# An expert kernel whose work is ordered by a list scheduler instead of by written times

## The chip, the core and the metric

The kernel runs on one core of one Trainium2 chip. The metric is the time of one execution on the device, in microseconds (us); a smaller number is better. Before the change, three runs took 2221.42 to 2222.93 us, with a median of 2222.36 us.

The core has five engines that matter here. TensorE (PE in the profile) multiplies matrices into PSUM. VectorE (DVE), ScalarE (ACT) and GpSimd (POOL) do the elementwise work. SyncE (SP) only issues transfers between HBM and SBUF here. Each engine works through its own queue strictly in the order in which the program issued its instructions, and waits on semaphores for the results of the others. So the order in which the program is written decides what an instruction that waits holds up behind it.

## What is computed

The reference is causal attention with a decay, then a dense mixture of experts, then a two-layer network. Cut to what matters:

```python
x = attention(q, k, v, f)            # 4 x 8 heads, 576 tokens each, head size 64 -> (2304, 512)
P = sinkhorn(exp(x @ w_gate), 8)     # 8 rounds of row and column normalisation, (2304, 8)
out = 0
for e in range(8):                   # every token goes through every expert
    h = maximum(x @ w1[e], 0)        # (2304, 1024)
    out += P[:, e:e+1] * (h @ w2[e])
h = out @ w_in                       # (2304, 2048)
return maximum(0.01 * h, h) @ w_out
```

All matrices are float32. The kernel keeps that precision by splitting each operand into a high and a low half and multiplying three times (high by high, high by low, low by high).

## The kernel before

Attention comes first, some 326 us long, and is the same in both versions. Into its gaps, and after it, go "fills": the products of the first four halves of experts for the first third of the tokens. What follows works on units.

**Units.** The tokens stand in three parts of 768, the hidden columns in groups of 512: 16 groups `g` for the experts (two per expert) and 4 for the last network (stage 1, from `GE` = 16 on). A unit is one part with one group, and there are 56 (part 0 skips the groups that the fills did). A unit's two matrix products are done by Strassen's scheme, so each layer takes 7 products of half size instead of 8: `p1` to `p7` for the first layer, `l1` to `l7` for the second. Each is 12 matmuls of 128x384 on TensorE. The products of unit u stand between the second-layer products of unit u-1, in the fixed order of `Q`: p1 p2 l1 p6 l2 l6 p7 p5 l5 l7 p3 p4 l3 l4. This order is the same after the change.

**Around the products.** ScalarE copies three products out of PSUM (`keep`, L1052), VectorE adds and applies the activation and the row of P (`c_add`, `act`, L1055 to L1071), GpSimd forms four sums (`s_sum`, L1078), ScalarE rounds each operand of the second layer to its high half (`op_hi`, L1083), VectorE subtracts to get the low half (`op_lo`, L1087), and the results are added into the accumulators (`evict`, L1095 on VectorE, L1093 on ScalarE for a first visit). Weights go the same way: raw load (L150), sums on VectorE (`w_sum`, L846), high half on ScalarE (L161), low half on GpSimd (L162). The operands of the first layer are made once per stage and part: four sums (`x_sum`, L774), seven high halves (`x_hi`, L777), seven low halves (`x_lo`, L781), then stores to HBM (`x_out`, L784 and L785); units load them back (`x_get`, L1014). For stage 1 they are made from the finished accumulators. The weights of the last network arrive as 64-bit words and are rewritten as float32 in 64 pieces (`conv_a`, L889 and L890; `conv_square`, L894; `conv_b`, L899 and L900).

**What sets the order.** Every event is entered with a time that its author computed from the nominal start of the products and a few durations, `at(t, key, name, fn, ..., need=...)`. At the end of the program each event is moved behind the last of its needs by a thousandth, and all are issued in order of these times:

```python
when[x] = max(when[x], last + 1e-3)
...
for t, x, key, name, fn, args, need in sorted(todo, key=lambda x: (when[x[2:4]], x[1])):
    fn(*args)
```

Nothing in this knows that an engine can do only one thing at a time, nor how long a transfer takes.

## Time and profile before

| | |
|---|---|
| median of three runs | 2222.36 us |
| the profiled execution, its own time | 2222.18 us |
| its span, first to last instruction | 2220.4 us |
| TensorE busy | 2055.6 us (93%) |
| VectorE busy | 1779.7 us (80%) |
| GpSimd busy | 1124.7 us (51%) |
| ScalarE busy | 984.0 us (44%) |
| the chain of work that ended last | TensorE 57%, VectorE 20%, GpSimd 7%, transfers 4% |

The profile is of one execution; its own time lies within the three runs. TensorE's share of busy time is an average over parts of the program with different limits. How much TensorE loses is read stage by stage: from the length of a stretch against the work in it.

### The profile page before, as it was taken

To read this page: it belongs to the slowest core of one execution; us is meant where nothing else is said; L and a number is where in the kernel's file an instruction comes from. 1 tells how busy PE (TensorE), PEld (TensorE's weight loads), DVE (VectorE), ACT (ScalarE), POOL (GpSimd) and SP (SyncE) were. 2 spreads that over 40 slices of the span, in tenths; PEclk is the share of its full clock that TensorE was granted. 3 is DMA by queue.
4 is the path that set the end of the run, shared out by engine and by line. 5 is a ranking of instruction groups with operands and counts; after the bars stand their busy time and mean duration, and the time that the engine had idled before them with its cause. 6 is when DMAs were issued, how large, how long until landed. Compare 5 with 4: busy or idle time off the path is not lost.

```text
span 2220.4 us, 32472 instructions
## 1 busy us (share of the span) xinstructions
PE 2055.6 (93%) x11760; PEld 1974.8 (89%) x11760; DVE 1779.7 (80%) x2257; ACT 984.0 (44%) x1784; POOL 1124.7 (51%) x709
## 2 busy tenths in 40 slices
PE   7999997699899999999999999999999877988998
PEld 6888886589889999999899999999999867888998
DVE  6789856487878888988889889889888766889656
ACT  7888854254333333333333333333333334544443
POOL 4676644376545545445454454543545445444531
PEclk9999999899999999999999999999999988999999
DMA  5655535857766676666676676766666777666653
GB/s 137 167 150 152 138 108 192 302 180 241 277 248 227 235 243 227 234 234 228 232 234 219 241 234 224 247 237 222 235 214 239 256 257 257 218 232 238 217 196 133
DMA packets 153798, 482.87 MB, mean 217 GB/s; under 512 B 16824, under 2 KB 43080, under 8 KB 153640
## 3 DMA queue, kind: packets, MB, share of 16 engines
q1 hardware_dynamic: 153640, 480.80, 64.0%
q8 instruction: 94, 1.54, 0.3%
q14 instruction: 64, 0.52, 0.1%
HBM read 424.78 MB, written 51.22 MB: 214 GB/s over the span
## 4 chain that ended last, share of the span: by engine, by line
PE 57%; DVE 20%; issue 8%; POOL 7%; DMA 4%; ACT 3%; SPq 1%; POOLq 0%; DVEq 0%; ACTq 0%
PE x L1027 28%; PE y L1027 18%; DVE acc_C L1095 3%; DVE wr L846 3%; PE ps_pv L529 3%; POOL w L162 3%; DVE hl L1087 2%; POOL s L1078 2%; PE ps_m L228 2%; PE ps_t L493 2%; POOL k L1078 1%; PE ps_m L201 1%; DVE u L1069 1%; DVE y L1055 1%; PE ps_s L441 1%
## 5 line engine op out<-in xcount | busy, mean ns | idle before, releaser
L162 POOL TENSOR_TENSOR w<-wr,w 128x512 fp32r<-128x512 f32 x288 | 417.8, 1456 | 457.0 <-ACT w L161 402.1
L1027 PE MATMUL x<-hh,w 128*128 128x384 f32 x1792 | 508.9, 345 | 80.2 <-DVE acc_C L1095 56.4
L1027 PE MATMUL x<-xw,w 128*128 128x384 f32 x2676 | 512.1, 340 | 13.2 <-ACT u L1052 4.5
L1027 PEld LDWEIGHTS x<-xw,w 128*128 128x128 f32 x2676 | 475.1, 191 | 23.2 <-ACT u L1052 10.8
L1027 PEld LDWEIGHTS x<-hh,w 128*128 128x128 f32 x1792 | 336.4, 193 | 95.3 <-DVE acc_C L1095 56.3
L1027 PE MATMUL y<-xw,w 128*128 128x384 f32 x2004 | 379.7, 337 | 18.1 <-DVE u L1058 16.2
L1027 PEld LDWEIGHTS y<-xw,w 128*128 128x128 f32 x2004 | 350.6, 189 | 25.2 <-DVE u L1058 23.0
L1027 PE MATMUL y<-hh,w 128*128 128x384 f32 x1344 | 368.4, 334 | 0.0
L1027 PE MATMUL x<-hl,w 128*128 128x384 f32 x896 | 306.2, 342 | 1.6 <-DVE hl L1087 1.6
L1078 POOL TENSOR_TENSOR k<-k,u 128x768 f32<-128x768 f32 x55 | 102.2, 1858 | 348.0 <-DVE u L1069 262.5
L1027 PEld LDWEIGHTS y<-hh,w 128*128 128x128 f32 x1344 | 245.1, 188 | 0.2 <-DVE acc_C L1095 0.2
L1027 PE MATMUL y<-hl,w 128*128 128x384 f32 x672 | 224.6, 334 | 0.0
L161 ACT ACTIVATE w<-wr 128x512 fp32r<-128x512 f32 x288 | 178.2, 622 | 75.5 <-PE y L1027 33.2
L1083 ACT ACTIVATE hh<-c 128x768 fp32r<-128x768 f32 x112 | 94.3, 842 | 217.8 <-PE y L1027 101.6
L1095 DVE TENSOR_TENSOR acc_C<-y,acc_C 128x768 f32<-128x768 f32 x148 | 140.6, 950 | 53.2 <-PE y L1027 53.2
L1095 DVE TENSOR_TENSOR acc_C<-x,acc_C 128x768 f32<-128x768 f32 x178 | 168.9, 949 | 9.9 <-PE x L1027 9.3
L1027 PEld LDWEIGHTS x<-hl,w 128*128 128x128 f32 x896 | 173.4, 194 | 2.0 <-DVE hl L1087 2.0
L1052 ACT ACTIVATE u<-x 128x768 f32<-128x768 f32 x112 | 91.0, 812 | 173.3 <-DVE hl L1087 137.4
L1083 ACT ACTIVATE hh<-u 128x768 fp32r<-128x768 f32 x112 | 94.1, 840 | 126.0 <-PE y L1027 108.6
L1087 DVE TENSOR_TENSOR hl<-u,hh 128x768 fp32r<-128x768 f32 x112 | 121.6, 1085 | 32.1 <-ACT hh L1083 32.1
L1087 DVE TENSOR_TENSOR hl<-s,hh 128x768 fp32r<-128x768 f32 x56 | 95.4, 1704 | 59.1 <-ACT hh L1083 58.9
L1087 DVE TENSOR_TENSOR hl<-c,hh 128x768 fp32r<-128x768 f32 x112 | 136.9, 1222 | 4.9 <-ACT hh L1083 2.6
(222 smaller groups left out, 3546.6 us busy)
## 6 DMA issues: line engine op xcount, KB each, us to landing
xw<-xo_t SPq DMA_DIRECT2D x224, 768.0 KB
xw<-xo_b SPq DMA_DIRECT2D x166, 768.0 KB
wr<-in_w_dram SPq DMA_DIRECT2D x88, 512.0 KB
pb<-prow SPq DMA_DIRECT2D x44, 384.0 KB
rq<-in_qT_dram SPq DMA_DIRECT2D x64, 144.0 KB
rk<-in_kT_dram SPq DMA_DIRECT2D x64, 144.0 KB
...
```

What stands on the lines that cost most here:

```text
L161: nc.scalar.activation(hv, src, AF.Copy)
L162: nc.gpsimd.tensor_tensor(lv, src, f(hv), ALU.subtract)
L228: nc.tensor.matmul(ps, h_[:, ts], w_, start=(x == 0), stop=(x == 11))
L493: nc.tensor.transpose(ps[:KV[j], c:c + m], prb[n, i][:m, j * P:j * P + KV[j]], ident[:m, :m])
L529: nc.tensor.matmul(ps[:, a - ra:rb - ra], vp, s[:KV[j], o:o + rb - a], start=(x == 0), stop=(x == len(todo) - 1))
L846: nc.vector.tensor_tensor(o, x, y, op)
L1027: nc.tensor.matmul(o_, w[:, k, w_], m[:, k, :], start=a and k + y == 0, stop=z and k == 1 and y == 2, skip_group_check=True)
L1052: nc.scalar.activation(ctile(u, name, name, bufs), pview(u, p), AF.Copy)
L1078: (nc.vector if u == NU - 1 else nc.gpsimd).tensor_tensor(tmp[u, o], tmp[u, a], tmp[u, b], op)
L1083: nc.scalar.activation(hi, tmp[u, LSRC[l]], AF.Copy)
L1087: nc.vector.tensor_tensor(lo, tmp[u, LSRC[l]], f(hi), ALU.subtract)
L1095: nc.vector.tensor_tensor(a, pview(u, l), a, ALU.add)
```

## The change

The times written for each event are replaced by a description of what the event is. `ev` takes an engine and a duration (`how`), all events that must come first (`need`), and events whose start it must follow (`after`). The letters are M for TensorE, A for ScalarE, V for VectorE, P for GpSimd and D for the transfers; "VP" marks a VectorE operation that can't run beside one on GpSimd, and a second pair in `how` lets the scheduler choose the engine. `run_events` computes a due time for every event backwards from the nominal places of the products. Then it walks forward through a model of five engines: it takes the candidate that can start first, looks past it to a more urgent one that becomes ready within its length, and issues the program in the order so found. The products keep their order among themselves.

Some events are cut finer or placed elsewhere. A fill's matmuls and the two halves of its rounding are events of their own. The high and low halves of the weights are two events. The loads of x of parts 1 and 2 have no need and so come at the start of this phase, part 1 first (before: part 2 at the start, part 1 some 34 us ahead of the first unit, after all stores of part 2). GpSimd may take any sum or low half of x. Of the 64 conversion pieces 48 instead of 40 lie in the stretch of units 9 to 41, evenly spaced, and 16 instead of 24 behind.

```diff
-    todo = []
-
-    def at(t, key, name, fn, *args, need=()):
-        todo.append((t, len(todo), key, name, fn, args, need))
-
-    HOP = 0.15
+
+
+
+    ENG = dict(V=nc.vector, P=nc.gpsimd)
+    TM, TMF1, TMF2 = 2.08, 0.70, 0.89
+    VX = ("V", 0.97)
+    VS = ("VP", 0.98)
+    VF = ("VP", 0.98, "P", 1.9)
+    AX_ = ("A", 0.85)
+    PX = ("P", 1.88)
+    DX = ("D", 1.95)
+    HOP, LAND = 0.13, 2.0
+    LOOK = dict(A=1.0, V=1.0, P=1.0, D=1.0)
...
+    def run_events():
...
+        for x, (_, _, _, need, after, _, _) in evs.items():
+            if evs[x][5] > noms[0]:
+                after.append(line[min(bisect_left(noms, evs[x][5]), len(line) - 1)])
...
+        due = {}
+        for x in reversed(topo):
+            how, due_ = evs[x][0], evs[x][6]
+            d = place.get(x, 1e9 if due_ is None else due_)
+            if x not in place:
+                for y, hard in succ[x]:
+                    lag = how[1] + HOP + (LAND if how[0] == "D" else 0.0) if hard else 0.0
+                    d = min(d, due[y] - lag)
+            due[x] = d
...
+        def offer(x):
+            how, _, _, need, after, t, _ = evs[x]
+            r = 0.0
+            me = how[0][0]
+            for n in need:
+                e = ran[n]
+                r = max(r, over[n] + (LAND if e == "D" else 0.0) + (0.03 if e == me else HOP))
+            for n in after:
+                r = max(r, at_[n])
+            for e in how[0::2]:
+                cand[e[0]][x] = (r, due[x], e == "VP" or e == "P")
+
...
+        order = []
+        while len(order) < len(evs):
+            best = None
+            for e in free:
+                here = []
+                for x, (r, d, p) in cand[e].items():
+                    if e == "M" and x in place and x != line[nl[0]]:
+                        continue
+                    s_ = max(r, free[e])
+                    if p:
+                        s_ = max(s_, port["P" if e == "V" else "V"])
+                    here.append((s_, e == "M" and x in place, d, e == "P", x))
+                if not here:
+                    continue
+                here.sort(key=lambda k: k[:4])
+                k = here[0]
+                if e in LOOK:
+
+                    for y in here[1:]:
+                        long = dur_of(k[4], e)
+                        if y[2] < k[2] and y[0] < k[0] + LOOK[e] * long and y[2] + slip[0] < k[0] + long:
+                            k = y
+                if best is None or k[:4] < best[0]:
+                    best = (k[:4], k[4], e)
+            k, x, e = best
+            how = evs[x][0]
+            if e == "M":
+                if x in place:
+                    nl[0] += 1
+                    slip[0] = k[0] - place[x]
+            for c in cand.values():
+                c.pop(x, None)
+            dur = dur_of(x, e)
+            at_[x], ran[x] = k[0], e
+            over[x] = free[e] = k[0] + dur
+            if how[0] == "VP" or e == "P":
+                port[e] = over[x]
+            order.append(x)
+            for y, _ in succ[x]:
+                left[y] -= 1
+                if not left[y]:
+                    offer(y)
+        for x in order:
+            how, fn, args = evs[x][:3]
+            fn(*args, *((ran[x],) if len(how) > 2 else ()))
 
...
+            need = [made[m] for m in XFROM[n]] + [(X, m) for m in XOVER[n]]
+            ev(X, n, VF if flex else VS, x_sum, stage, part, n, need=need)
+            made[n] = (X, n)
+        for n in XOPS:
+            to = (lambda n=n: xlo[n]) if n in near else (lambda: None)
+            ev(X, "h " + n, AX_, x_hi, stage, part, n, need=[made[n]] + list(free.get(n, ())))
+            ev(X, "l " + n, VF if flex else VS,
+               lambda *e, n=n, to=to: x_lo(stage, part, n, to(), *(e or ("V",))),
                need=[(X, "h " + n)] + [(X, m) for m in XLAST[n]])
...
+            ev(X, "o " + n, DX, lambda n=n, to=to: x_out(stage, part, n, to()), need=[(X, "l " + n)])
...
-    T0X = {2: 1.0, 1: base - 34.0}
-    for part in (2, 1):
-        t0, X = T0X[part], ("x", 0, part)
-        was = lambda n, m=None: [(("x", 0, 2), "o " + n)]
-        pre = [(("x", 0, 2), "o " + n) for n in XOPS] if part == 1 else []
-        at(t0, X, "load", x_load, part, BLK, need=[("start", "places")] + pre)
-        free = dict(t3=[(X, "o b11")], t1=[(X, "o b21")], b22=[(X, "o t2")], t4=[(X, "o t3")])
-        if part == 1:
-            free = dict(b22=[(X, "o t2")], t4=[(X, "o t3")])
-        x_events(0, part, t0 + 4.0, {n: (t0 + 4.0, (X, "load")) for n in BLK},
-                 4.5 if part == 2 else 2.6, free, "vvpvpvp")
...
+    for part in (1, 2):
+        X = ("x", 0, part)
+        for n in ("b11", "b12", "b21", "b22"):
+            ev(X, "load " + n, ("D", 1.1), lambda part=part, n=n: x_block(part, n, xat[0, part][n]))
+        free = dict(t2=[], t3=[], t1=[], b22=[(X, "o t2")], t4=[(X, "o t3")])
+        if part == 2:
+            was = lambda n: [(("x", 0, 1), "o " + n)]
+            free = dict(b11=was("b22"), b21=was("t4"), t2=was("t1"), t3=[(X, "o b11")],
+                        t1=[(X, "o b21")], b22=[(X, "o t2")], t4=[(X, "o t3")])
+        x_events(X, True, free, {n: (X, "load " + n) for n in BLK}, ("b11", "b21") if part == 1 else ())
+        if part == 2:
+            for n in ("t2", "t3", "t4"):
+                evs[X, n][3].extend(was(n))
...
-    cu = []
-    for u in range(9, U2 - 2):
-        cu += [(u, 0)] + ([(u, 1)] if u % 5 == 0 else [])
-    for u in range(U2 + 2, U2 + 8):
-        cu += [(u, x) for x in range(5)]
-    for j, (u, x) in enumerate(cu[:64]):
...
+    n1 = 48
+    for j in range(64):
+        ct.append(unit0[9] + span * j / n1 if j < n1 else unit0[U2 + 2] + 8.0 * (j - n1))
...
-        at(ta - 8.0, C, "load", conv_load, j, need=need)
-        at(ta, C, "a", conv_a, j, need=[(C, "load")])
-        at(ta + 2.0, C, "square", conv_square, j, need=[(C, "a")])
-        at(ta + 6.1, C, "b", conv_b, j, need=[(C, "square")])
...
+        ev(C, "load", ("D", 0.75), conv_load, j, need=need, t=ct[j] - 8.0)
+        ev(C, "a", ("V", 0.72), conv_a, j, need=[(C, "load")], t=ct[j])
+        ev(C, "square", ("A", 0.4), conv_square, j, need=[(C, "a")])
+        ev(C, "b", ("V", 0.86), conv_b, j, need=[(C, "square")])
+        ev(C, "store", ("D", 0.4), conv_store, j, need=[(C, "b")])
...
+                need = [dep(d) for d in WDEP[str(x)]] + [(G, f"raw {which}")]
+                need += w_free(14 * g + 7 * which + x)
+                ev(G, f"{nm}hi {x}", ("A", 0.64), w_high, g, which, x, need=need, after=[wlast],
+                   t=t_ + gap * x)
+                ev(G, f"{nm}lo {x}", ("P", 1.3), w_low, g, which, x, need=[(G, f"{nm}hi {x}")])
+                wlast = (G, f"{nm}hi {x}")
...
+                ev(G, f"{nm}s{x}", ("VP", 0.7), w_sum, g, which, x, need=need)
...
+        need = [(("x", g // GE, part), "o " + XN[p])] + ([lastf[0]] if x < XR else [loads[x - XR]])
+        after = [(loads[x - 1][0], "x " + loads[x - 1][1])] if x else []
+        ev(u, "x " + p, DX, x_get, u, p, need=need, after=after)
...
-            at(E_[u, l] + HOP, key, "e " + l, evict, u, l, need=need)
...
+            if g not in (0, GE) or l in ("l2", "l3", "l7"):
+                need += [(key, "e " + dict(l2="l1", l3="l6", l7="l5").get(l, l))] if l in ("l2", "l3", "l7") else []
+            first = g in (0, GE) and l in ("l1", "l6", "l5", "l4")
+            ev(key, "e " + l, AX_ if first else VX, evict, u, l, need=need,
+               due=E_[u, l] + 3.0)
...
-    for t, x, key, name, fn, args, need in sorted(todo, key=lambda x: (when[x[2:4]], x[1])):
-        assert did.issuperset(need), (key, name, need)
-        fn(*args)
-        did.add((key, name))
```

**ScalarE at the end of the fills**, as the queue of before holds it. `hh<-` are the high halves that a fill's second layer waits for; the rows from `xu_4897` to `xc_4900<-acc_C_1_4876` are the seven high halves of x of part 1.

```order
L166 ACTIVATE hh<-y_5271 128x384
L973 ACTIVATE acc<-acc,prob 128x512
L161 ACTIVATE w<-wr 128x512
L777 ACTIVATE xu_4897<-acc_C_1_4873 128x768
L777 ACTIVATE xs_4899<-acc_C_1_4874 128x768
L777 ACTIVATE acc_C_0_4871<-spare_4882 128x768
L777 ACTIVATE acc_C_0_4872<-acc_C_1_4875 128x768
L777 ACTIVATE xc_4900<-spare_4881 128x768
L777 ACTIVATE acc_C_0_4871<-spare_4883 128x768
L777 ACTIVATE xc_4900<-acc_C_1_4876 128x768
L166 ACTIVATE hh<-x_5298 128x384
L166 ACTIVATE hh<-y_5360 128x384
```

The same place after the change (`L902` is `x_hi`, `L214` the fill's high half, `acc_C_2` belongs to part 2):

```order
L1093 ACTIVATE acc<-acc,prob 128x512
L1075 ACTIVATE pr<-x_5212 72x256
L1093 ACTIVATE acc<-acc,prob 128x512 x2
L163 ACTIVATE w<-wr 128x512
L1093 ACTIVATE acc<-acc,prob 128x512 x3
L902 ACTIVATE xc_4887<-acc_C_1_4876 128x768
L214 ACTIVATE hh<-y_5278 128x384
L902 ACTIVATE xc_4887<-acc_C_2_4877 128x768
L214 ACTIVATE hh<-x_5297 128x384
L214 ACTIVATE hh<-y_5317 128x384
L214 ACTIVATE hh<-x_5335 128x384
L163 ACTIVATE w<-ws 128x512
```

Before, seven halves of x stand in one block ahead of two fills; after, the halves of part 1 are mostly earlier, and one of part 1 and one of part 2 stand between fills.

**VectorE in the slot of unit 18**, a typical one in the long middle. Before: `L1095` adds a product into an accumulator, `L1087` is a low half, `L889` and `L890` are a conversion's first two operations, `L1055` and `L1069` belong to p2; the row with `x_10391` for `acc_C_0_4871` is the one that l1 of the unit before gives, and that l6 waits for.

```order
L1095 TENSOR_TENSOR acc_C_2_4878<-y_10237,acc_C_2_4878 128x768
L1087 TENSOR_TENSOR hl<-c_10327,hh 128x768
L1095 TENSOR_TENSOR acc_C_2_4879<-x_10117,acc_C_2_4879 128x768
L1087 TENSOR_TENSOR hl<-s_10342,hh 128x768
L889 TENSOR_SCALAR acc<-acc 128x256
L890 SCALAR_TENSOR_TENSOR acc<-acc 128x256
L1055 TENSOR_TENSOR y_10372<-y_10372,k_10389 128x2x384
L1069 SCALAR_TENSOR_TENSOR k_10389<-y_10372,pb 128x768
L1095 TENSOR_TENSOR acc_C_0_4871<-x_10391,acc_C_0_4871 128x768
L1087 TENSOR_TENSOR hl<-u_10173,hh 128x768
```

After (`L1217` adds, `L1209` is a low half, `L998` and `L999` are the conversion, `x_10398` is l1):

```order
L1217 TENSOR_TENSOR acc_C_2_4878<-y_10235,acc_C_2_4878 128x768
L998 TENSOR_SCALAR acc<-acc 128x256
L999 SCALAR_TENSOR_TENSOR acc<-acc 128x256
L1217 TENSOR_TENSOR acc_C_2_4879<-x_10121,acc_C_2_4879 128x768
L1008 SCALAR_TENSOR_TENSOR acc<-acc 128x256
L1009 SCALAR_TENSOR_TENSOR acc<-acc 128x256
L1209 TENSOR_TENSOR hl<-c_10328,hh 128x768
L1209 TENSOR_TENSOR hl<-s_10349,hh 128x768
L1177 TENSOR_TENSOR y_10376<-y_10376,k_10391 128x2x384
L1191 SCALAR_TENSOR_TENSOR k_10391<-y_10376,pb 128x768
L1217 TENSOR_TENSOR acc_C_0_4871<-x_10398,acc_C_0_4871 128x768
L1209 TENSOR_TENSOR hl<-u_10193,hh 128x768
```

The conversion has moved ahead of the last addition of the unit before, its second half (`L1008`, `L1009`) follows at once, and nothing of it stands any more between the low half for l6 (`hl<-s`) and the addition of l1.

**ScalarE at the border of the two stages**, in the slot of unit 45, from the copy of p1 on. Before: `L777` rows are high halves of x of part 2, `L1093` is the first visit of l1 to its accumulator.

```order
L1052 ACTIVATE k_17781<-x_17742 128x768
L777 ACTIVATE acc<-spare_4881 128x768
L1071 ACTIVATE k_17781<-y_17766 128x768
L777 ACTIVATE acc<-spare_4882 128x768
L1083 ACTIVATE hh<-u_17552 128x768
L1093 ACTIVATE acc_C_0_4871<-x_17789 128x768
L161 ACTIVATE w<-wr 128x512
```

After (`L902` is a high half of x, `L1215` the first visit):

```order
L1174 ACTIVATE k_17769<-x_17739 128x768
L902 ACTIVATE acc<-spare_4883 128x768
L1205 ACTIVATE hh<-s_17772 128x768
L1193 ACTIVATE k_17769<-y_17756 128x768
L1215 ACTIVATE acc_C_0_4871<-x_17777 128x768
L1205 ACTIVATE hh<-u_17588 128x768
L163 ACTIVATE w<-ws 128x512
```

Two high halves of x stood ahead of l1's first visit to its accumulator; now one does, the last of part 1, and behind it comes the high half for l6 (`hh<-s`).

## Rows read from the trace of the kernel before

**Rows 1.** The page: length of the profiled span.
```profile
span 2220.4 us, 32472 instructions
```
**Rows 2.** Stretches: length; busy PE, PEld, DVE, ACT, POOL; clock, DMA share, GB/s.
```profile
326.00:404.35 78.35, 53.12 (x259) 45.84 (x259) 45.18 (x91) 28.42 (x48) 32.59 (x21) 0.87 0.64 226
404.35:474.82 70.47, 57.40 (x292) 53.56 (x292) 48.27 (x44) 25.61 (x41) 38.52 (x23) 0.93 0.62 221
474.82:701.29 226.47, 213.57 (x1202) 210.32 (x1201) 176.77 (x183) 95.96 (x136) 132.02 (x79) 0.98 0.71 251
701.29:1741.41 1040.12, 1007.14 (x5713) 989.82 (x5713) 907.37 (x963) 374.72 (x538) 514.86 (x294) 1.00 0.67 232
1741.41:2051.51 310.10, 256.98 (x1345) 247.32 (x1345) 240.88 (x269) 136.36 (x203) 148.36 (x83) 0.92 0.70 242
2051.51:2168.04 116.53, 116.53 (x673) 116.53 (x673) 71.43 (x74) 52.13 (x67) 52.35 (x29) 1.00 0.60 209
```
**Rows 3.** What TensorE waited for, 326 to 474.82: total us, times, longest.
```profile
PE x L201 <- DVE hl L167: 17.8, 1, 17.8
PE x L1027 <- ACT hh L1083: 4.6, 1, 4.6
```
**Rows 4.** Timeline of ScalarE: start, length, instruction, idle time before it and its releaser.
```profile
398.24 0.84 ACT L777 ACTIVATE xc<-acc_C 128x768 fp32r<-128x768 f32 x1 [5.65 <-DMA xo_t<-xc]
398.99 0.47 ACT L166 ACTIVATE hh<-x 128x384 fp32r<-128x384 f32 x1
```
**Rows 5.** Timeline of TensorE around that wait.
```profile
380.41 2.38 PE L201 MATMUL y<-xp,w 128*128 128x384 f32 x12 [1.24 <-DVE hl L167]
400.60 3.92 PE L201 MATMUL x<-xp,w 128*128 128x384 f32 x12 [17.80 <-DVE hl L167]
```
**Rows 6.** What TensorE waited for, 701.29 to 1741.41.
```profile
PE x L1027 <- DVE acc_C L1095: 21.8, 26, 1.6
PE y L1027 <- DVE u L1058: 10.8, 14, 2.4
```
**Rows 7.** Timeline of VectorE in the slot of unit 18.
```profile
980.85 1.38 DVE L889 TENSOR_SCALAR acc<-acc 128x256 uint32<-128x256 uint32 x1
982.26 1.95 DVE L890 SCALAR_TENSOR_TENSOR acc<-acc 128x256 uint32<-128x256 uint32 x1
986.00 0.95 DVE L1095 TENSOR_TENSOR acc_C<-x,acc_C 128x768 f32<-128x768 f32 x1
```
**Rows 8.** Timelines of TensorE and GpSimd in the same slot.
```profile
987.00 0.45 PE L1027 MATMUL x<-hh,w 128*128 128x384 f32 x1 [0.95 <-DVE acc_C L1095]
980.06 2.02 POOL L162 TENSOR_TENSOR w<-wr,w 128x512 fp32r<-128x512 f32 x1
```
**Rows 9.** Lines L1087 and L889 over the span: shortest, median, longest in ns.
```profile
L1087 DVE TENSOR_TENSOR hl<-k,hh x112: 941/958/1769, 440.1 to 2206.4; 128x768 fp32r<-128x768 f32 x112
L1087 DVE TENSOR_TENSOR hl<-c,hh x112: 941/959/2677, 441.0 to 2208.5; 128x768 fp32r<-128x768 f32 x112
L1087 DVE TENSOR_TENSOR hl<-u,hh x112: 941/959/2132, 455.6 to 2210.5; 128x768 fp32r<-128x768 f32 x112
L1087 DVE TENSOR_TENSOR hl<-s,hh x56: 946/1714/2602, 449.6 to 2199.3; 128x768 fp32r<-128x768 f32 x56
L889 DVE TENSOR_SCALAR acc<-acc x64: 281/1378/1939, 705.9 to 2044.0; 128x256 uint32<-128x256 uint32 x64
```
**Rows 10.** What TensorE waited for, 1741.41 to 2051.51.
```profile
PE x L1027 <- DVE acc_C L1095: 23.1, 8, 7.3
PE x L1027 <- ACT acc_C L1093: 15.5, 2, 12.1
```
**Rows 11.** Timelines of the transfers' queue and of ScalarE, slot of unit 45.
```profile
1848.36 0.42 SPq L784 DMA_DIRECT2D xo_b<-acc  x1
1854.22 0.84 ACT L777 ACTIVATE acc<-spare 128x768 fp32r<-128x768 f32 x1 [4.18 <-DMA xo_b<-acc]
1855.70 0.79 ACT L1093 ACTIVATE acc_C<-x 128x768 f32<-128x768 f32 x1
```

More of the change, by code (lines that the diff above doesn't have):

```diff
@@ L1165, in moe_kernel @@
             if n == "f":
-                for y, fn in enumerate(fills[n_f][1]):
-                    at(t, "start", f"fill {n_f}" + (f" {y}" if y else ""), fn)
-                t += 0.87
-                at(t + 0.6, "start", f"fill {n_f} end", fill_end)
-                ends.append(t)
-                n_f += 1
+                p_ = moved.pop(0)
+                fixed.append((t, len(fixed), p_[2]))
+                t += TMF2
                 continue
@@ L1181, in moe_kernel @@
     unit0[NU + 1] = t
-    assert n_f == nf
-    tp_ = base + 0.5
-    at(tp_, "start", "prob t", prob_t, need=[("start", "cols 7")])
-    at(tp_ + 0.7, "start", "prob out", prob_out, need=[("start", "prob t")])
-    for i in range(TPP):
-        x = nf - 1 - 3 * (TPP - 1 - i) - (3 * FC if i < TPB else 0)
-        at(ends[x] + 3.0, "start", f"scale {i}", acc_scale, i,
-           need=[("start", "cols 7"), ("start", f"fill {x} end")])
+    assert not moved
+    st = [f(cp.tile([P, 2, TB], F32R, tag=n, name="x" + n, bufs=b)) for n, b in
+          (("u3", 2), ("u3", 2), ("s2", 1), ("c21", 1), ("u2", 1))]
@@ L1400, in moe_kernel @@
-    done = set()
-    def settle(x, path=()):
-        assert x not in path, path
-        if x not in done:
-            last = max((settle(n, path + (x,)) for n in needs[x]), default=-1e9)
-            when[x] = max(when[x], last + 1e-3)
-            done.add(x)
-        return when[x]
-    for _, _, key, name, _, _, _ in todo:
-        settle((key, name))
-    did = set()
-    for t, x, key, name, fn, args, need in sorted(todo, key=lambda x: (when[x[2:4]], x[1])):
-        assert did.issuperset(need), (key, name, need)
-        fn(*args)
-        did.add((key, name))
+                ev(key, "put " + n, ("D", 1.1), put, part, n, need=[(key, "e " + l)])
@@ L1419 @@
+    run_events()
 _OUTS = [((DM, N), "float32")]
```

517 lines of the change are left out of this document (291 added, 226 removed).

## The prediction

> **What bounds the kernel now.** I read the page's header first, then the busy time by stretch, then what TensorE waited for in each stretch, and last the timelines around the longest waits. The span is 2220.4 us [rows 1], and the execution took 2222.18 us, so 1.8 us lie outside it. The three runs shown have a median of 2222.36 us, 0.2 us from the profiled one, so sums against the profile carry over as they are.
>
> The table by stretch [rows 2] is the key. Its last row is four units in which TensorE is busy for 116.53 of 116.53 us at full clock: a unit without any stall is 116.53 / 4 = 29.13 us. The products and their order on TensorE don't change, so no unit gets shorter than that. The gap of each other stretch is its length less the work in it:
>
> - A, end of attention and fills (326 to 404): 78.35 - 53.12 busy = 25.2 us idle, and a slow restart: twelve matmuls of a fill took 3.92 us after the long wait against 2.38 us earlier [rows 5], 1.5 us. Gap 26.7.
> - B, first two units with the last fills: 70.47 long, 57.40 busy at a mean clock of 0.93. The work at full clock is about 57.40 x 0.93 = 53.4. Gap 17.1.
> - C, units 2 to 8: 226.47 - 7 x 29.13 = 22.6.
> - D, units 9 to 42: 1040.12 - 34 x 29.13 = 49.7, or 1.46 per unit.
> - E, units 43 to 50 at the border of the stages: 310.10 - 8 x 29.13 = 77.1.
>
> Together 193.2 us, so with every gap closed the time is 2222.2 - 193.2 = 2029. Only these gaps are at stake; attention and the last units are left alone.
>
> **The change part by part.** Each term has the same bounds from the rows: at best its whole gap goes, at worst nothing does; a loss is possible too and has its own bound below (VectorE), so it is not repeated at each term.
>
> *A.* TensorE waited 17.8 us in one wait for a fill's low half on VectorE [rows 3]. VectorE was not the cause: its operand, the high half on ScalarE, ran at 398.99, right behind the last high half of x, which had itself waited 5.65 us for a store [rows 4]. Seven high halves of x stood ahead of two fills' halves in one queue, and the x halves wait for stores to free their buffers. After, they are spread between the fills, the raw x comes earlier, and at the last fills one half of part 1 and one of part 2 remain. The latter reuses a buffer that a store must leave first. The planner allows such a transfer 1.95 + 2.0 = 3.95 us; the trace shows 1848.36 to 1854.22 = 5.9 us from issue to release [rows 11]. What is late next is this half, by 5.9 - 3.95 = 2 us. The other 7.4 us of idle time are short waits such as the 1.24 us of [rows 5]; I leave 3. Gain 26.7 - 5 = about 22.
>
> *B.* Here the waits are for the same family of halves (4.6 us once [rows 3]) while the x work of part 2 goes on beside two units. The planner sees both, but not the true length of a transfer. I keep a third: gain 17.1 - 5.6 = 11.5. A restart at a lower clock goes with the wait before it.
>
> *C.* The same x work thins out here. By D's rate after the change (below, 0.6 per unit) 4.2 would remain; the x halves that go on beside these units make it twice that. Gain 22.6 - 8.6 = 14.
>
> *D.* TensorE waited 26 times, 21.8 us in all, for an addition on VectorE (L1095), the one of l1 that l6 must follow, and 14 times, 10.8 us, for a sum in the first layer [rows 6]. In unit 18 the cause stands in the timeline: a conversion's two operations, 1.38 and 1.95 us, run ahead of the addition at 986.00 [rows 7], and TensorE starts at 987.00 after 0.95 us of waiting [rows 8]. The new order puts the conversion ahead of the previous unit's last addition, and nothing of it between the low half for l6 and l1's addition. So the 21.8 go where a conversion was in the way. What is queued behind it now is that last addition and the low halves for l2 and l6; and the conversion's second half waits for ScalarE's square. With the second half no longer than the first (3.33 us, my bound), a piece delays them by 6.7 us. l2 is the fifth product of the slot, so four products of 29.13 / 14 = 2.08 us, 8.3 us, lie before it: covered by 1.6 us. If that cover fails, a wait of 1 to 2 us comes back per piece, 48 to 96 us over 48 pieces at the extreme; the gap before the change (1.46 per unit) speaks against it. The stretch also gets 48 pieces instead of 40: 8 x 6.7 / 34 = at most 1.6 us more of VectorE per unit on 907.37 / 34 = 26.7, so 28.3, still below 29.13. That leaves little slack, so I don't take all: of 1.46 per unit 0.6 stays. 34 x 0.6 = 20 stay; gain 49.7 - 20 = 30.
>
> The plan books a conversion's first operation with its second, at 0.72 us, as a plain VectorE event; the row has a median of 1.378 for the first alone, and a shortest of 0.281 [rows 9]. The long ones lie beside GpSimd's work: in unit 18 a weight's low half of 2.02 us ran from 980.06 [rows 8] over the 1.38 at 980.85 [rows 7]. The Trainium skill, "SBUF — State Buffer", section "Who interferes with whom", says that a VectorE operation with two SBUF inputs contends with a GpSimd operation that reads SBUF, that one in a two-port mode (a tensor_scalar can be) contends too, and that the later one then blocks for the whole instruction; these rows agree. By that rule the pieces stay long wherever the plan lets them run beside GpSimd, which is the reason for what I leave, and rival 2 if it spreads.
>
> *E.* Two things add up. ScalarE's first visit of l1 stood behind two high halves of x of which one waited 4.18 us for a store [rows 11]; TensorE waited 15.5 us in two such waits, and 23.1 in eight for the additions on VectorE [rows 10]. VectorE was busy for 240.88 / 8 = 30.1 us per unit [rows 2], over the 29.13 that TensorE needs: it bounds this stretch. After, 8 pieces fewer lie here, 8 x 3.33 to 8 x 6.7 = 27 to 54 us off VectorE, 23 to 27 us per unit, and GpSimd may take sums and low halves of x. The first visit has one x half ahead of it instead of two. What is left: the new operands of parts 1 and 2 are still stored and loaded back for units 44 to 46 with a true 5.9 us where 3.95 is planned, 2 us each, and a unit has p2 and p6 early in it to wait for this: 2 x 2 x 3 = 12 us; as much again for the lower clock (0.92) after stalls and for VectorE's bunching. Gain 77.1 - 25 = 52.
>
> *At nothing:* the early x loads (as many bytes as before; transfers were busy for 0.60 to 0.71 of every stretch [rows 2]; if they do delay weights, that shows in C), the finer events (the same instructions), the products' order.
>
> Sum: 22 + 11.5 + 14 + 30 + 52 = 129.5. 2222.2 - 129.5 = 2092.7, say 2093 us. Halving or raising what I leave (64 us) by one half gives 2061 and 2125; the likeliest case's own range is 2050 to 2130.
>
> **Rivals.**
>
> 1. *The plan's transfers and conversions are too short, and the stalls stay in another place.* For: 5.9 us against 3.95 for a store; a conversion of 3.33 against 0.72. If a store and the load behind it each take 8.2 instead of 3.95 (an estimate, 5.9 plus another 40% for the busier queue), each chain of the border is late by 8.5 us, for two operands in each of three units 51 us. Then E gains nothing but the 26 beside it, and D keeps 40 of its 49.7. Gains 22 + 11.5 + 0 + 10 + 26 = 69.5: 2153 us. Against: units can be late once and stay so, without paying each link. The Trainium skill, "DMA: Bandwidth & Descriptors", section "Anatomy of one DMA — SWDGE (gpsimd) path", prices a transfer that GpSimd issues at about 2.0 us fixed plus its bytes over 436 GB/s; my estimate by it, for a store that SyncE issues here, for the two 384 KB halves of one operand is 3.8 us, what the plan has. The 5.9 us measured decide against that.
>
> 2. *Slower: VectorE becomes the bound of the long middle.* The plan keeps marked VectorE operations and GpSimd's apart, but only in its own clock; on the chip nothing holds them apart, and a new order with more on GpSimd can lay them on each other. A unit's seven low halves take 2 x 0.958 + 2 x 0.959 + 2 x 0.959 + 1.714 = 7.5 us by the medians and 2 x 1.769 + 2 x 2.677 + 2 x 2.132 + 2.602 = 15.8 by the longest [rows 9], 8.3 more. VectorE would then be busy for 26.7 + 8.3 = 35.0 us per unit and set the pace: D grows by 34 x (35.0 - 30.6) = 150, against 99.5 gained elsewhere: 2222 - 99.5 + 150 = 2273 us. It decides from 30.6 + 99.5 / 34 = 33.5 us of VectorE per unit on. Against: the medians stand at the shortest times in three of four forms, so overlap is rare today, and TensorE's own order limits how far things move.
>
> 3. *Nearly all goes:* the plan's slack covers transfers, and 10 us remain: 2040 us. For: units 51 to 54 run without any stall. Against: VectorE's 26.7 to 28.3 of 29.13 us in D.
>
> That the change does not do what it says is excluded by the order of the instructions: at each of the three places what stood ahead has moved.
>
> **How the numbers follow.** Forecast 0.65, rival 1 0.19 (2130 to 2215), rival 2 0.10, rival 3 0.04, no change 0.02. A difference under 0.2%, 4.4 us, is about what a measurement of this kernel can't tell from no change. Faster: 0.65 + 0.19 + 0.04 less 0.01 of rival 1's upper end = 0.87; within 0.2% 0.03; slower 0.10. The range takes the forecast's, rival 3 from 2040, and rival 1 to a little beyond its centre, 2165: what is left out is 0.10 + 0.08.
>
> **What would show it.** A: no wait over 4 us for a fill's low half. B, C: stretches of about 59 and 212 us. D: 34 units in about 1010 us, waits for L1095's successor under 8 us in all; VectorE under 28.5 us busy per unit. E: about 258 us, no wait over 3 us behind ScalarE's first visit, what remains ending with transfers of x. A D stretch over 1040 us with VectorE above 30 us per unit would be rival 2; an E stretch over 280 us with waits that transfers end would be rival 1; four-unit stretches at 29.2 us per unit in D rival 3.

## The result and the profile after

The changed kernel takes 2098.71 us (median of four runs, 2094.43 to 2100.48) against 2221.89 us for the kernel before (four runs, 2220.80 to 2222.93): a ratio of 0.9443, 95% interval 0.9426 to 0.9459. The profiled execution has a span of 2097.7 us, 122.7 less than [rows 1].

Busy time by stretch after, cut at the same events as [rows 2] (columns as there): up to unit 0, units 0 and 1, 2 to 8, 9 to 42, 43 to 50, 51 to 54, and the end.

```profile
326.00:375.71 49.71, 49.02 (x269) 44.98 (x268) 33.26 (x77) 23.64 (x42) 32.07 (x20) 1.00 0.71 248
375.71:434.17 58.46, 52.63 (x290) 50.35 (x290) 43.55 (x46) 26.97 (x39) 33.86 (x21) 1.00 0.93 351
434.17:651.15 216.98, 209.86 (x1202) 205.98 (x1202) 191.49 (x176) 95.27 (x135) 145.16 (x84) 1.00 0.75 262
651.15:1658.10 1006.95, 995.61 (x5714) 989.39 (x5713) 927.95 (x1003) 388.77 (x556) 524.07 (x304) 1.00 0.70 243
1658.10:1931.48 273.38, 248.46 (x1345) 242.92 (x1345) 216.02 (x231) 134.92 (x193) 151.52 (x84) 0.96 0.77 266
1931.48:2047.96 116.48, 116.48 (x673) 116.48 (x673) 75.81 (x77) 52.89 (x68) 51.22 (x31) 1.00 0.59 204
2047.96:2097.70 49.74, 44.09 (x253) 43.48 (x252) 32.62 (x35) 15.91 (x19) 4.67 (x2) 0.99 0.37 128
```

The differences of the lengths give the account: A and B together 148.8 to 108.2 (40.6 us gained), C 226.5 to 217.0 (9.5), D 1040.1 to 1007.0 (33.2), E 310.1 to 273.4 (36.7), and 2.6 at the end of the program. They sum to 122.6. VectorE's work did not shrink: 1777.5 us against 1779.7, in a shorter time.

The waits of TensorE after, in D (651.15 to 1658.10) and then in E; columns: engine, tile and line that waited, what for, total us, times, longest. Lines of the changed kernel: L1149 is a unit's matmul, L1217 and L1215 the additions, L1209 the low half, L1174 ScalarE's copy.

```profile
PE x L1149 <- DVE hl L1209: 4.1, 4, 1.6
PE x L1149 <- ACT u L1174: 3.8, 3, 2.3
PE x L1149 <- DVE acc_C L1217: 2.2, 6, 0.7
PE x L1149 <- DVE acc L1217: 0.6, 1, 0.6
```

```profile
PE x L1149 <- DMA xw<-xo_t: 10.1, 5, 2.7
PE x L1149 <- ACT u L1174: 3.8, 3, 2.1
PE y L1149 <- DVE u L1180: 2.9, 1, 2.9
PE x L1149 <- ACT w L163: 2.8, 1, 2.8
PE x L1149 <- DVE acc_C L1217: 2.6, 2, 2.1
PE y L1149 <- DMA xw<-xo_b: 1.0, 2, 0.6
```

Against [rows 6] the 21.8 us for the addition are 2.2 (2.8 with the first accumulator's), and the 10.8 us for the first layer's sum are gone. Against [rows 10] the 15.5 us behind ScalarE's first visit are gone, and 23.1 us for the additions are 2.6; 11.1 us for loads of x stand in their place. From 326 us to unit 2 the 17.8 us of [rows 3] are gone; the longest wait there is 3.4 us, for a load of x.

In place of the wait of [rows 7, 8], here is a slot of D after the change, that of unit 20, in which TensorE doesn't wait: VectorE, then GpSimd (start, length, instruction, idle time before it; three short rows between the second and the third of VectorE are left out).

```profile
981.36 1.22 DVE L998 TENSOR_SCALAR acc<-acc 128x256 uint32<-128x256 uint32 x1 [1.47 <-DMA acc<-in_w_in_dram]
982.61 1.95 DVE L999 SCALAR_TENSOR_TENSOR acc<-acc 128x256 uint32<-128x256 uint32 x1
986.45 0.95 DVE L1191 SCALAR_TENSOR_TENSOR k<-y,pb 128x768 f32<-128x768 f32 x1
987.32 0.95 DVE L1217 TENSOR_TENSOR acc_C<-x,acc_C 128x768 f32<-128x768 f32 x1
988.18 0.95 DVE L1209 TENSOR_TENSOR hl<-s,hh 128x768 fp32r<-128x768 f32 x1
```

```profile
980.58 1.85 POOL L1200 TENSOR_TENSOR u<-u,u 128x768 f32<-128x768 f32 x1
982.38 1.89 POOL L1200 TENSOR_TENSOR c<-c,s 128x768 f32<-128x768 f32 x1
```

The conversion's first half is about as long as before (1.22 + 1.95) and still beside GpSimd; its second half, in the rows left out, takes 0.65 + 0.42. What has moved in this slot is the low half for l6, `hl<-s`: it stands behind l1's addition, at a time when GpSimd's sums are over, and takes 0.95 us. In D this is so in 19 of 34 units (0.99 us on average). In the other 15 it still stands ahead, as in unit 18:

```profile
925.48 0.95 DVE L1209 TENSOR_TENSOR hl<-s,hh 128x768 fp32r<-128x768 f32 x1
928.22 0.95 DVE L1217 TENSOR_TENSOR acc_C<-x,acc_C 128x768 f32<-128x768 f32 x1
```

It takes more than 1.1 us in 4 of these 15 and in 2 of the 19; in the kernel before it stood ahead of that addition in all 34 and took 1.72. The conversions have moved too: before, an operation of one stood between this low half and l1's addition in 33 of 34 slots, after in 4. TensorE's waits of over 0.2 us for l1's addition went from 20.0 us to 0.7.

### The profile page after: what moved, and what is told of

It reads as the page before. It is cut to its first block, busy times and chain, and to the rows that moved or that the text cites. A ratio compares the mean times of both kernels' runs of the same rounds, so it can differ in the third digit from the quotient of the medians.

```text
span 2097.7 us, 32576 instructions
## 1 busy us (share of the span) xinstructions
PE 2021.5 (96%) x11760; PEld 1959.8 (93%) x11760; DVE 1777.5 (85%) x2242; ACT 993.3 (47%) x1784; POOL 1144.2 (55%) x724
## 4 chain that ended last, share of the span: by engine, by line
PE 74%; DVE 13%; DMA 6%; issue 3%; ACT 2%; SPq 1%; POOL 1%; DVEq 0%; ACTq 0%; POOLq 0%
PE x L1149 35%; PE y L1149 26%; PE ps_pv L534 3%; DVE hl L1209 2%; PE ps_m L233 2%; PE ps_t L498 2%; DVE acc_C L1217 2%; DMA xo_t<-spare 1%; PE ps_m L206 1%; DMA acc<-in_w_in_dram 1%; DVE acc L999 1%; DMA xw<-xo_t 1%; PE ps_s L446 1%; DVE acc L998 1%; PE ps_s L447 1%
## 5 line engine op out<-in xcount | busy, mean ns | idle before, releaser
L167 POOL TENSOR_TENSOR w<-wr,w 128x512 fp32r<-128x512 f32 x288 | 431.5, 1508 | 306.2 <-ACT w L163 265.0
L1149 PE MATMUL x<-xw,w 128*128 128x384 f32 x2676 | 508.5, 338 | 30.4 <-DMA xw<-xo_t 12.6
L1149 PEld LDWEIGHTS x<-xw,w 128*128 128x128 f32 x2676 | 471.9, 190 | 37.3 <-ACT u L1174 14.4
L1149 PE MATMUL x<-hh,w 128*128 128x384 f32 x1792 | 493.7, 336 | 8.0 <-DVE acc_C L1217 6.0
L1149 PE MATMUL y<-xw,w 128*128 128x384 f32 x2004 | 376.7, 335 | 3.9 <-DVE u L1180 2.9
L1149 PE MATMUL y<-hh,w 128*128 128x384 f32 x1344 | 369.3, 335 | 0.0
L1149 PEld LDWEIGHTS y<-xw,w 128*128 128x128 f32 x2004 | 350.7, 188 | 5.3 <-DVE u L1180 3.6
L1149 PEld LDWEIGHTS x<-hh,w 128*128 128x128 f32 x1792 | 327.6, 188 | 12.9 <-issue 4.9
L1149 PE MATMUL x<-hl,w 128*128 128x384 f32 x896 | 301.0, 336 | 6.8 <-DVE hl L1209 6.7
L1149 PEld LDWEIGHTS y<-hh,w 128*128 128x128 f32 x1344 | 246.6, 189 | 0.0
L1149 PE MATMUL y<-hl,w 128*128 128x384 f32 x672 | 225.4, 335 | 1.2 <-DVE hl L1209 1.2
L1217 DVE TENSOR_TENSOR acc_C<-y,acc_C 128x768 f32<-128x768 f32 x148 | 140.8, 951 | 62.8 <-PE y L1149 62.4
L1217 DVE TENSOR_TENSOR acc_C<-x,acc_C 128x768 f32<-128x768 f32 x178 | 169.3, 951 | 29.1 <-PE x L1149 27.7
L1149 PEld LDWEIGHTS x<-hl,w 128*128 128x128 f32 x896 | 168.6, 188 | 9.6 <-DVE hl L1209 9.6
L1174 ACT ACTIVATE u<-x 128x768 f32<-128x768 f32 x112 | 91.0, 813 | 148.1 <-DVE hl L1209 88.1
L167 POOL TENSOR_TENSOR w<-ws,w 128x512 fp32r<-128x512 f32 x40 | 53.4, 1335 | 187.2 <-ACT w L163 178.6
L1209 DVE TENSOR_TENSOR hl<-c,hh 128x768 fp32r<-128x768 f32 x112 | 141.7, 1266 | 3.5 <-ACT hh L1205 3.3
L1200 POOL TENSOR_TENSOR c<-c,s 128x768 f32<-128x768 f32 x55 | 117.0, 2127 | 44.2 <-DVE hl L1209 37.7
```

Of the source, the lines that this page charges most:

```text
L167: nc.gpsimd.tensor_tensor(lv, src, f(hv), ALU.subtract)
L1149: nc.tensor.matmul(o_, w[:, k, w_], m[:, k, :], start=a and k + y == 0, stop=z and k == 1 and y == 2, skip_group_check=True)
L1174: nc.scalar.activation(ctile(u, name, name, bufs), pview(u, p), AF.Copy)
L1200: ENG["V" if u == NU - 1 else "P"].tensor_tensor(tmp[u, o], tmp[u, a], tmp[u, b], op)
L1209: nc.vector.tensor_tensor(lo, tmp[u, LSRC[l]], f(hi), ALU.subtract)
L1217: nc.vector.tensor_tensor(a, pview(u, l), a, ALU.add)
```

## The experiments

Theory Q, with which I began: the order keeps what waits from standing ahead of what TensorE needs. Its rivals: the early load of x (X), the eight moved conversions (C), and the rule that keeps marked VectorE operations and GpSimd apart (P).

**x loaded late, as before.** The list scheduler stays, the order and needs of the loads go back:

```diff
-    for part in (1, 2):
+    for part in (2, 1):
         X = ("x", 0, part)
+        pre = outs(0, 2) if part == 1 else []
...
+               need=pre, t=base - 34.0 if part == 1 else 0.0)
```

> The changed kernel, but x of parts 2 and 1 is loaded in the order and with the needs of the kernel before: part 2 at the start, part 1 some 34 us ahead of the first unit and after all stores of part 2. Theory Q (what gains is that the planner puts no instruction that waits ahead of one that TensorE needs): the planner works around the late x too; the stretches from 326 us to unit 2 (148.8 us before, 108.2 after) take 108 to 118 us, the whole 2099 to 2109 us. Rival X (the early load of part 1 is what gained there): they take 133 us or more, the whole 2124 us or more.

Measured 2102.07 us (ratio to before 0.9461, 0.9447 to 0.9475; the changed kernel's is 0.9443, 0.9426 to 0.9459). The two stretches up to unit 2, now cut at 380.50 and 443.30:

```profile
326.00:380.50 54.50, 49.82 (x268) 44.78 (x267) 38.44 (x84) 27.04 (x47) 29.79 (x19) 1.00 0.70 242
380.50:443.30 62.80, 54.88 (x289) 51.61 (x289) 42.21 (x47) 24.64 (x37) 34.45 (x23) 0.97 0.89 328
```

117.3 us, 9 more than after the change, of which units 2 to 8 give 5.5 back. Rival X falls: the planner makes 31.5 of the 40.6 us of A and B with the old load order too.

**The conversions alone, in the kernel before**, 48 and 16 instead of 40 and 24:

```diff
-        cu += [(u, 0)] + ([(u, 1)] if u % 5 == 0 else [])
+        cu += [(u, 0)] + ([(u, 1)] if u % 2 == 0 and u > 10 else [])
...
-        cu += [(u, x) for x in range(5)]
+        cu += [(u, x) for x in (0, 2, 4)]
```

> The kernel before, with written times, but 48 conversion pieces in the stretch of units 9 to 41 and 16 behind, as after the change. Theory Q: the order is what counts, so units 43 to 50 fall only from 310 to about 290 us, since ScalarE's head-of-line waits stay, and units 9 to 42 rise from 1040 to about 1050: 2205 to 2215 us in all. Rival C (the moved pieces gave the gain at the border): units 43 to 50 fall to 275 to 280 us and the whole to 2185 to 2195.

Measured 2223.70 us (ratio 1.0008, 0.9999 to 1.0018). D and E of this kernel:

```profile
700.39:1754.51 1054.12, 1011.36 (x5714) 992.97 (x5714) 925.01 (x995) 378.67 (x546) 514.74 (x294) 1.00 0.66 232
1754.51:2050.65 296.14, 251.01 (x1345) 243.92 (x1345) 221.76 (x231) 132.69 (x193) 148.97 (x83) 0.93 0.69 240
```

E gives 14.0 us, D takes 14.0 back: with written times, no gain. Neither theory had D's price right (I had said 10).

**The reverse: 40 and 24 in the changed kernel.**

```diff
-    n1 = 48
+    n1 = 40
...
-        ... unit0[U2 + 2] + 8.0 * (j - n1))
+        ... unit0[U2 + 2] + 6.0 * (j - n1))
```

> The changed kernel with 40 conversion pieces in units 9 to 41 and 24 behind (6 us apart), as before the change. Theory Q: units 43 to 50 take 273 + 5 to 15 us, units 9 to 42 some 3 us less than 1007: 2100 to 2110 us in all. Rival C: units 43 to 50 go back most of the way to 310 us: 2125 us or more.

Measured 2097.00 us (ratio 0.9436, 0.9422 to 0.9450), no different from the change; D takes 1003.55 and E 267.80, and units 51 and 52 are 5.6 us longer together. Rival C falls twice. Theory Q missed here as well: it had E 5 to 15 us longer.

**Planned without the rule for VectorE and GpSimd.**

```diff
-                cand[e[0]][x] = (r, due[x], e == "VP" or e == "P")
+                cand[e[0]][x] = (r, due[x], False)
```

> The changed kernel, planned without the rule that keeps the marked operations of VectorE and GpSimd apart; all else is as in the changed kernel. Theory Q (the drift between plan and chip undoes that rule anyway): within 5 us of 2099. Rival P (the rule is what makes the long middle tight, the slower case of the prediction avoided by it): units 9 to 42 take 1024 us or more instead of 1007, VectorE is busy for 29 us or more per unit there, 2116 us or more in all.

Measured 2132.74 us (ratio 0.9598, 0.9583 to 0.9612): 34 us of the gain are gone, 25 of them in D. That ends theory Q's "within 5 us".

```profile
658.81:1690.91 1032.10, 1004.21 (x5713) 994.54 (x5713) 938.01 (x995) 382.96 (x546) 520.62 (x294) 0.99 0.69 237
```

```profile
PE x L1149 <- DVE acc_C L1217: 24.5, 14, 3.3
```

One of these waits, on VectorE, GpSimd and TensorE:

```profile
996.25 1.89 DVE L1209 TENSOR_TENSOR hl<-s,hh 128x768 fp32r<-128x768 f32 x1 [0.63 <-ACT hh L1205]
998.06 2.06 DVE L1008 SCALAR_TENSOR_TENSOR acc<-acc 128x256 uint32<-128x256 uint32 x1
1000.23 1.33 DVE L1009 SCALAR_TENSOR_TENSOR acc<-acc 128x256 f32<-128x256 f32 x1
1001.48 0.95 DVE L1177 TENSOR_TENSOR y<-y,k 128x768 f32<-128x768 f32 x1
1002.47 0.96 DVE L1191 SCALAR_TENSOR_TENSOR k<-y,pb 128x768 f32<-128x768 f32 x1
1003.35 0.95 DVE L1217 TENSOR_TENSOR acc_C<-x,acc_C 128x768 f32<-128x768 f32 x1
```

```profile
995.30 2.02 POOL L1200 TENSOR_TENSOR u<-u,u 128x768 f32<-128x768 f32 x1
997.29 2.56 POOL L1200 TENSOR_TENSOR c<-c,s 128x768 f32<-128x768 f32 x1
```

```profile
1004.35 0.44 PE L1149 MATMUL x<-hh,w 128*128 128x384 f32 x1 [2.91 <-DVE acc_C L1217]
```

The low half for l6 is back ahead of l1's addition (in all 34 units, 1.74 us on average) and runs beside GpSimd's sums. But it isn't alone there: the second half of a conversion, 2.06 + 1.33 us, stands between it and the addition. And only 7 of the 14 waits (10.8 us) are for l1's addition. The other 7 (13.8 us) are for the last addition of the unit before, with no low half for l6 among the eight VectorE operations ahead of it, as here:

```profile
1300.36 1.88 DVE L1009 SCALAR_TENSOR_TENSOR acc<-acc 128x256 f32<-128x256 f32 x1
1303.03 1.72 DVE L1209 TENSOR_TENSOR hl<-c,hh 128x768 fp32r<-128x768 f32 x1
1305.77 0.41 PE L1149 MATMUL x<-hh,w 128*128 128x384 f32 x1 [2.34 <-DVE acc_C L1217]
```

In all 14, operations of a conversion are among these eight, and the eight together are longer than the shortest of their kinds by 1.9 to 6.0 us, each time by more than TensorE waits (0.5 to 3.3). So long operations ahead of an addition account for the waits; which of them decides, the low halves or the conversions, isn't shown. Rival P's time came, but not by its mechanism: VectorE is busy for 938.01 / 34 = 27.6 us per unit against 27.3 after the change, not 29. What the rule changes is where the long operations fall. The Trainium skill, "SBUF — State Buffer", section "Who interferes with whom", says that a VectorE operation with two SBUF inputs contends with a GpSimd operation that reads SBUF. The 1.89 here against 0.95 above agrees.

**The two places by hand, in the kernel before.** Two late x halves go between the next fills' halves, and each unit's first conversion goes around the last addition of the unit before, as [rows 4, 7] suggested:

```diff
-            th = max(th, t[n][0] + HOP)
+            th = max(th, t[n][0] + HOP) + (14.0 if X == ("x", 0, 1) and n == "b22" else 0.0)
...
+        if u < U2 and not x:
+            ta -= 4.2
...
-        at(ta + 2.0, C, "square", conv_square, j, need=[(C, "a")])
-        at(ta + 6.1, C, "b", conv_b, j, need=[(C, "square")])
+        at(ta + (1.0 if u < U2 and not x else 2.0), C, "square", conv_square, j, need=[(C, "a")])
+        at(ta + (2.2 if u < U2 and not x else 6.1), C, "b", conv_b, j, need=[(C, "square")])
```

> The kernel before, with written times, and two moves by hand: two high halves of x of part 1 (b22 and t4) go behind the next fills' halves on ScalarE, and the first piece of each unit's conversions, both halves, stands ahead of and behind the last addition of the unit before, as in the changed kernel (nothing of it between the low half for l6 and l1's addition). Theory Q (these places are the gain of their stretches): 326 us to unit 2 takes 128 to 136 us instead of 148.8, units 9 to 42 1012 to 1025 instead of 1040: 2180 to 2197 us in all. Rival H (a wait that goes by hand comes back as the next one, since GpSimd's sums still run beside the low half for l6): units 9 to 42 take 1032 us or more, 2203 us or more in all.

Measured 2245.98 us (ratio 1.0112, 1.0093 to 1.0132): 1.1% longer than before, clear of the measurement's uncertainty. D's stretch and its waits, and the first waits from 326 us to unit 2:

```profile
702.23:1766.58 1064.35, 1014.85 (x5713) 997.45 (x5713) 963.66 (x963) 378.15 (x538) 495.85 (x294) 0.99 0.64 227
```

```profile
PE x L1027 <- DVE acc_C L1095: 41.1, 23, 2.3
```

```profile
PE x L201 <- DVE hl L167: 10.1, 1, 10.1
PE x L1027 <- ACT hh L1083: 5.0, 1, 5.0
PE x L1027 <- ACT k L1052: 3.6, 1, 3.6
```

The 17.8 us became 10.1, unit 0 starts 6.5 us sooner, and unit 2 at 475.96 instead of 474.82: all given back in units 0 and 1. In D the waits for the addition nearly doubled, since l1 now waits too, and VectorE's busy time rose by 963.66 - 907.37 = 56 us. Theory Q as I had it, a gain that lies in these places, falls: nothing of a conversion stands between the low half for l6 and l1's addition in any of the 34 slots, and TensorE still waits. Rival H's times came. Of the 23 waits 11 (20.7 us) are for l1's addition, behind a conversion's second half and this low half, and 12 (20.4 us) for the last addition of the unit before, behind the conversion's first half and another low half. One of each, without the short operations between:

```profile
737.50 1.33 DVE L900 SCALAR_TENSOR_TENSOR acc<-acc 128x256 f32<-128x256 f32 x1
738.75 2.05 DVE L1087 TENSOR_TENSOR hl<-s,hh 128x768 fp32r<-128x768 f32 x1
797.89 2.01 DVE L890 SCALAR_TENSOR_TENSOR acc<-acc 128x256 uint32<-128x256 uint32 x1
800.69 1.74 DVE L1087 TENSOR_TENSOR hl<-c,hh 128x768 fp32r<-128x768 f32 x1
```

In all 23 the eight operations ahead of the addition are again longer than the shortest of their kinds by more than the wait. The two moves were run together; their stretches are disjoint, but what each does to E (1.6 us longer) or to the end isn't separated.

**Without looking past the first candidate.**

```diff
-    LOOK = dict(A=1.0, V=1.0, P=1.0, D=1.0)
+    LOOK = {}
```

> The changed kernel, planned without looking past the first candidate to a more urgent one: each engine takes what can start first. Theory Q (the gain is that urgent work isn't held up behind work that waits or isn't urgent): half or more of the 123 us goes, 2160 us or more. Rival G (that nothing waits ahead of ready work is all that counts, and starting what can start first has that already): 2099 to 2115 us.

Measured 2110.35 us (ratio 0.9493, 0.9479 to 0.9507): 12 us by the medians. Of the profiled executions, 8.0 us apart, units 2 to 8 lose 12.8 (229.80 us against 216.98) and the stretch ahead of them 2.6; D is 2.0 shorter (1004.96) and E 5.6 (267.74). Rival G holds and theory Q's 2160 falls: a model in which an engine takes what can start first has nine tenths of the gain.

**The length of a transfer in the plan: 0, 4 and 6 us instead of 2.** E still takes 273.4 - 233.0 = 40.4 us more than eight units without a stall. TensorE is idle for 24.9 of them (273.38 - 248.46), of which 11.1 are waits for loads of x, all in units 44 to 46; the other 15.4 (248.46 - 233.0) are matmuls that run longer, at a mean granted clock of 0.96. In unit 44 the transfers' queue and TensorE show a chain of a store and the load behind it:

```profile
1685.56 0.68 SPq L910 DMA_DIRECT2D xo_t<-acc  x1
1690.01 4.10 SPq L1136 DMA_DIRECT2D xw<-xo_t  x3
```

```profile
1696.20 3.46 PE L1149 MATMUL x<-xw,w 128*128 128x384 f32 x12 [2.58 <-DMA xw<-xo_t]
```

From the issue of the first of these loads, the one that TensorE waits for, to TensorE's start are 6.2 us; the plan has 1.95 + 2.0. The twelve matmuls behind the wait take 3.46 us, against 2.24 in the slot of unit 20. The edit, with 4.0 (and 0.0, 6.0):

```diff
-    HOP, LAND = 0.13, 2.0
+    HOP, LAND = 0.13, 4.0
```

> The changed kernel, planned with the transfer that its trace shows: 4.0 us from the end of a transfer's issue to its release instead of 2.0 (5.95 in all; 5.9 measured). Theory T (what is left at the border, 40 us over 8 full units, is a plan that counts on x too early and so makes it too late): units 43 to 50 take 255 to 263 us instead of 273, the whole 2080 to 2090. Rival L (the chain of additions, halves, store and load of x at the border is as short as the buffers let it be; the plan can't start it sooner): the same waits for x loads, within 5 us of 2099.

> The changed kernel, planned with 0.0 us instead of 2.0 from the end of a transfer's issue to its release. Theory T (the border's remainder is the plan's error in a transfer's length): units 43 to 50 get longer, 280 us or more, the whole 2106 us or more. Rival R (that 4.0 gave 2075 is one lucky order among many of like length): 2085 to 2104, either side of 2099.

> The changed kernel, planned with 6.0 us, 2 more than the trace has. Theory T with the true length as the best: 2075 to 2092 us. Rival M (any early due time for transfers helps, the more the better): below 2070 us. Rival R (luck): 2092 us or more.

| LAND | median us | ratio to before | units 43 to 50, us |
|---|---|---|---|
| 0.0 | 2141.55 | 0.9645 (0.9628 to 0.9661) | 296.09 |
| 2.0 (the change) | 2098.71 | 0.9443 (0.9426 to 0.9459) | 273.38 |
| 4.0 | 2075.16 | 0.9336 (0.9322 to 0.9350) | 249.26 |
| 6.0 | 2077.91 | 0.9354 (0.9340 to 0.9368) | 249.83 |

With 4.0 the waits in E for loads of x are

```profile
PE x L1149 <- DMA xw<-xo_t: 2.4, 2, 1.6
```

and with 0.0 the first two rows of that kind are

```profile
PE y L1149 <- DMA xw<-xo_t: 10.0, 2, 5.1
PE x L1149 <- DMA xw<-xo_t: 7.8, 5, 3.2
```

Theory T holds: of the four planned lengths, each one nearer the measured one makes E shorter, and the one beyond it changes E by 0.6 us; L, M and R fall. In size T was too careful: it had 255 to 263 us for E and 2080 to 2090 in all with 4.0. Of E's 24.1 us, 13.2 are idle time of TensorE (24.9 to 11.7), and 10.9 faster matmuls (248.46 to 237.56 us busy, mean granted clock 0.96 to 0.99). With 0.0 only 22.7 of the 42.8 us lost lie in E; units 2 to 8 lose 12.9. The chain could start sooner; the plan didn't know that it had to. With 4.0 the kernel is the fastest of this study, 146.7 us below before.

**The conversions marked as not beside GpSimd, alone and with 4.0.**

```diff
-        ev(C, "a", ("V", 0.72), conv_a, j, need=[(C, "load")], t=ct[j])
+        ev(C, "a", ("VP", 0.72), conv_a, j, need=[(C, "load")], t=ct[j])
...
-        ev(C, "b", ("V", 0.86), conv_b, j, need=[(C, "square")])
+        ev(C, "b", ("VP", 0.86), conv_b, j, need=[(C, "square")])
```

> The changed kernel, with the conversion's operations on VectorE marked as ones that can't run beside GpSimd, as the low halves are. Theory P (the conversions beside GpSimd, 1.0 to 1.7 us instead of 0.28 to 0.43 each, make most of what the long middle still loses): units 9 to 42 take 995 to 1002 us instead of 1007, the whole 2086 to 2094. Rival N (they already stand where VectorE has slack, and the extra rule moves other work): within 4 us of 2099 or slower.

> The changed kernel with both, the longer transfer in the plan and the conversions marked. If theories T and P hold, their gains add up: 2070 to 2082 us. If L and N hold: 2094 to 2105 us.

Alone 2095.06 us (ratio 0.9428, 0.9405 to 0.9450), with 4.0 2094.42 (0.9425, 0.9409 to 0.9441). Alone, D is 999.16 us, as theory P said, and VectorE's work there falls to 864.42 us; but the total is within the measurement's uncertainty of the change, as rival N said. A new wait of 5.6 us for a low half, in unit 43 with the last of these pieces and the first of x, doesn't explain it, since E is 3.0 us shorter all the same (270.38). The profiled execution is the shortest of the four (2090.32), so where the median loses D's 7.8 us stays open. With 4.0, D is 1007.62 and E 257.57: the gains don't add, and 19 us of LAND's 23.5 are lost. The total is what theory N had, whose partner L had fallen. Why this plan comes out worse I didn't settle.

**Lengths from the trace for other operations, with 4.0.**

```diff
-    PX = ("P", 1.88)
+    PX = ("P", 2.03)
...
-        ev(C, "a", ("V", 0.72), ...
+        ev(C, "a", ("V", 1.8), ...
-        ev(C, "b", ("V", 0.86), ...
+        ev(C, "b", ("V", 1.75), ...
-                ev(G, f"{nm}lo {x}", ("P", 1.3), ...
+                ev(G, f"{nm}lo {x}", ("P", 1.5), ...
```

> The changed kernel with 4.0 us for a transfer and with mean lengths from its trace: a conversion's two halves 1.8 and 1.75 us instead of 0.72 and 0.86, GpSimd's sums 2.03 instead of 1.88, the weights' low halves 1.5 instead of 1.3. Theory T+ (the nearer the plan's lengths, the better): units 2 to 42 take 1215 us or less (1222.6 with 4.0 alone), the whole 2055 to 2068. Rival S (lengths below a microsecond don't decide; the order changes at random): 2070 to 2095.

Measured 2093.31 us (ratio 0.9424, 0.9410 to 0.9438), 18 more than with 4.0 alone; units 2 to 42 take 1238.2 us. Theory T+ falls; the time lies in rival S's range. VectorE is busy for 962.06 us in D here, against 927.30 with 4.0 alone. My reading, that a mean which holds collisions is not what the next plan will meet, isn't tested, and the four lengths were changed together. This run and the one with the conversions marked and 4.0 show that a small change of the plan can move the total by 18 to 19 us for no reason that I know.

## Why the prediction was right, and where not

The time lies 5.7 us above the forecast of 2093, inside the likeliest case's own range. By its terms:

- **A and B**: 33.5 forecast, 40.6 measured. The wait that I read, x halves with open waits ahead of fills, is gone, and what still waits there are loads of x, 5.9 us in two waits. But that this one cause makes the gain isn't shown: two of these halves moved by hand took 7.7 us off the wait and nothing off the time to unit 2. The other parts of the change that act here, fills cut finer and GpSimd taking sums and low halves of x (33 of them over the program instead of 18), were not run by themselves.
- **C**: 14 forecast, 9.5 measured; waits for low halves, ScalarE's copies and weights are left (6.8 us together), none of them named in the prediction.
- **D**: 30 forecast, 33.2 measured, 0.49 left per unit where I had 0.6. The size was right, the step only half. I put the gain on the conversion's new place, and the waits for l1's addition did go with it. But the kernel moved by hand has nothing of a conversion at the old place either and loses 24 us in D: the new place alone is not the gain. Its 23 waits, 0.9 to 2.3 us each, are about what I had foreseen for the case that the slack of 1.6 us fails, and had set aside. What keeps them away in the changed kernel includes the port rule, worth 25 us of D, which I had only as a danger (rival 2); by which operation it does so isn't shown. VectorE stayed at 27.3 us per unit, far from the 33.5 from which rival 2 would decide, and under 28.3.
- **E**: 52 forecast, 36.7 measured, the mis-sized term. What stays is 40.4 instead of 25. The waits for loads of x themselves are 11.1 us, near the 12 that I had for transfers. Too small is the rest, for which I took "as much again", 13: it is 29.3, of which 15.4 are slower matmuls and 13.8 other waits. Much of it hangs on the transfers all the same, as rival 1 had it (3.95 planned, 5.9 measured): with 4.0 in the plan the waits for x fall to 2.4 us and E by 24.1. I had VectorE bound this stretch; it didn't: its 30.1 us per unit stood in a stretch of 310.10 / 8 = 38.8, and over 29.13 they explain 8 us of the 77.1. The moved conversions were to take 27 to 54 us off it; all changes together took 24.9 (240.88 to 216.02). Moved alone they were worth 14.0 us of E in the kernel before, and moved back nothing in the changed one.
- **At nothing**: the early loads, costless as said: with the old loads the kernel is 3 us slower, with intervals that overlap.

The sum was good partly because errors cancel: 10.3 us more gained in A, B and D and 2.6 at the end stand against 19.8 less in C and E.
